# A weight's low three bits: from VectorE's shift-and-merge to a rounded product on GpSimd

## The chip, the cores and the metric

One core of one Trainium2 chip runs the whole program. The metric is the device time of one execution in microseconds, the median over several runs. All times below are in microseconds unless they are marked ns.

## The reference

A causal, exponentially decaying linear attention (no softmax) is followed by a feed-forward layer whose activation is a rational function. Cut to what is computed:

```python
# q, k, v: (8, 8, 576, 64) float32
scores = scale * q @ k^T
ret    = scores * where(rel >= 0, gamma_h ** rel, 0)      # per head
x      = (ret @ v) -> (4608, 512)
# w_in: (512, 2048), w_out: (2048, 512), both float64
h = x @ w_in
g = (a0 + a1*h + a2*h^2 + a3*h^3) / (1 + |b0|*|h| + |b1|*h^2 + 1e-6)
out = (g @ w_out) as float32
```

The weights arrive as float64, eight bytes each, and have to be turned on the chip into numbers that the matmuls can use.

## The kernel before

The 4608 tokens are cut into 36 units of 128 tokens for the attention part and into 9 blocks (`b`) of 512 tokens for the feed-forward part. The feed-forward part runs over 16 slices (`f`) of 128 hidden columns. For each pair (b, f), a *step*, TensorE does `gemm1` (12 matmuls of 128x512 into a PSUM tile `h`) and, three or four steps later, `gemm2` (12 matmuls into accumulators `acc`). Each product of two float32 numbers is made of three products of float32r parts, a high and a low one, which is why each weight tile `w` has two halves.

Between the two matmul groups lies the elementwise work of a step: on ScalarE `ffn_p` (two activations, p and u), `ffn_va`, `ffn_r` (Ln and Exp) and `ffn_hi`; on VectorE a product and a fused product in `ffn_p`/`ffn_p2`, then `ffn_v`, `ffn_q` (two operations) and `ffn_q3`; the low half of g (`ffn_lo`) is made by GpSimd in the first 24 steps and by VectorE later. u lies in SBUF, but in 13 of the first 24 steps it lies in a PSUM tile named `free_at`.

The weights are converted once, by `split_weight`, for 32 slices (16 of `w_in`, 16 of `w_out`). A slice arrives as a tile `bits` of 128 x 512 64-bit words, of which `low` and `high` are the two 32-bit words (every second word). `split_weight` is a generator with four cuts, so that its parts can be spread over the schedule: at `start` ScalarE makes c from the high word by an Abs with a scale; at `split0`, `split1` and `split2` VectorE shifts and merges bits into c; at `split3` ScalarE writes the high half of `w` and GpSimd subtracts it from c for the low half.

The order of the instructions of each engine is the order of the program. It is written out by hand in lists of names, of which `run` calls one after the other:

```python
FIRST = (
    "split1 gemm1 visit ffn_p split2 ffn_p2 ffn_hi decay keep_hi ffn_lo gemm2 ffn_r scale_q split3 decay1 add fade keep_lo"
    " start scale_v split0 ffn_q ffn_q3 ffn_va ffn_v"
).split()
MID = (
    "split1 split2 gemm1 ffn_p ffn_r ffn_hi ffn_lo split3 ffn_va gemm2 ffn_p2 ffn_q ffn_v ffn_q3 start split0"
).split()
```

The stages in order of time: *before* (attention units 0 to 4, ending with the list `LAST_BEFORE`, which ends "split2 split3 split0"; six slices are started there, three of them at its end); steps 0 to 7 and 21 to 23 by `FIRST`; steps 8 to 20 by `MID`; later steps, by other lists, start no slice. `STARTS_BEFORE = [0, 1, 1, 1, 3]` and `STARTS = [1, 1, 2, 1, 2] + [1] * 19` say how many slices are started in each. GpSimd's own order in a step of `FIRST` is `ffn_lo` (tile g), `scale_q` (tile qk, only where a unit follows), `split3` (tile w), `fade` (tile S, only with a unit).

All instructions are recorded by one helper, so that nearly all rows of the profile have its line, L73; they are told apart by their tiles.

Of the kernel before, what the change touches and what calls it, by code (L numbers as in the profile page):

```python
# [15 lines left out]
U32 = mybir.dt.uint32  # L16
I64 = mybir.dt.int64
AF = mybir.ActivationFunctionType
ALU = mybir.AluOpType
# [57 lines left out]
def retention_ffn(ctx: ExitStack, tc: tile.TileContext, qkv, w_in, w_out, ab, masks, gq, gv, out):  # L77
# [26 lines left out]
    pe, act, dve, pool = (InOrder(tc, e) for e in (nc.tensor, nc.scalar, nc.vector, nc.gpsimd))  # L104
# [48 lines left out]
    def split_weight(k):  # L153


        nm = f"{k[0]}_{k[1]}"
        words = bits[k].bitcast(I32).rearrange("p (c w) -> p c w", w=2)
        low, high = words[:, :, 0], words[:, :, 1]
        c = cnv.tile([P, DM], I32, tag="c", name=f"c{nm}")
        cf = c.bitcast(F32)  # L160


        act.activation(cf, high.bitcast(F32), AF.Abs, scale=math.ldexp(1.0, -112))
        yield
        dve.tensor_scalar(c, c, 3, 1, ALU.logical_shift_left, ALU.bitwise_or)
        yield
        dve.scalar_tensor_tensor(c, low, 29, c, ALU.logical_shift_right, ALU.bitwise_or)
        yield
        dve.scalar_tensor_tensor(c, high, -0x80000000, c, ALU.bitwise_and, ALU.bitwise_or)
        yield  # L170
        w = wts.tile([P, 2, DM], F32R, tag=f"w{nm}", name=f"w{nm}")
        del bits[k]
        act.activation(w[:, 0, :], cf, AF.Copy)
        pool.tensor_tensor(w[:, 1, :], cf, w[:, 0, :].bitcast(F32), ALU.subtract)
        parts[k] = w
# [335 lines left out]
    def split_start(n):  # L511
        for k in [k for _, k in zip(range(n), splits)]:
            going.append([split_weight(k), 0])
            next(going[-1][0])
# [129 lines left out]
```

## Time and profile before

| | |
|---|---|
| median of 3 runs | 941.3 us (940.4 to 941.72) |
| the profiled execution: its time | 940.24 us |
| its span in the trace | 938.5 us |
| busy in the span | PE 899.4, DVE 825.0, ACT 710.2, POOL 153.0 us |
| mean clock granted to TensorE | 0.985 |

PE is TensorE's matmuls, PEld its weight loads, DVE is VectorE, ACT ScalarE, POOL GpSimd. In rows of the timeline the columns are the start, the duration, the engine, the line, the operation, output<-inputs, the shapes, the count (xN), and in brackets the idle time of the engine before it with what ended it. In rows of groups the columns after xN are busy time, mean ns of one, then idle time before them. In rows by stage, each engine has its busy time and (in brackets) the number of its instructions, then follow the granted clock of TensorE, the share of the DMA engines that was busy and GB/s.

### The profile page before, as it was taken

The page shows a single profiled execution, that of the slowest core. Times are in us where ns is not written, and L with a number is a line of the kernel's source. Part 1 is how long each engine was busy: PE and PEld are TensorE (multiplying, and loading weights), DVE is VectorE, ACT ScalarE, POOL GpSimd, SP SyncE. Part 2 cuts the span into 40 slices and gives each one's busy share as a digit, 9 for nine tenths or more (in the row PEclk, how much of TensorE's full clock was granted, in tenths as well). Part 3 has the DMA queues.
Part 4 walks back from the last instruction along what each step waited for, and adds up shares of the span by engine and source line. Part 5 has one row for each costly group of instructions (what it writes and reads, how often), then busy time and mean ns, then how long its engine had stood idle before and what let it go on. Part 6 is the DMA issues. An engine that isn't in the chain of part 4 may idle for free.

```text
span 938.5 us, 19369 instructions
## 1 busy us (share of the span) xinstructions
PE 899.4 (96%) x7852; PEld 737.2 (79%) x7852; DVE 825.0 (88%) x1252; ACT 710.2 (76%) x1274; POOL 153.0 (16%) x128
## 2 busy tenths in 40 slices
PE   6689889989999999999999999999999999999997
PEld 6567668877878888888888888888888888888886
DVE  3799999999888888888888999898888888888895
ACT  4567788887777777877787778777877787867775
POOL 3544344444100000000000000000000000000000
PEclk9789999989999999999999999999999999999999
DMA  9976000003212111211121112111211121001001
GB/s 341 362 276 203 1 0 1 1 13 124 91 46 87 49 36 32 84 40 41 43 90 45 47 46 91 45 47 46 90 46 46 45 91 47 1 1 45 1 1 45
DMA packets 20568, 65.50 MB, mean 70 GB/s; under 512 B 2432, under 2 KB 2432, under 8 KB 20480
## 3 DMA queue, kind: packets, MB, share of 16 engines
q1 hardware_dynamic: 20480, 64.28, 19.5%
q8 instruction: 61, 1.00, 0.4%
q14 instruction: 27, 0.22, 0.1%
HBM read 54.83 MB, written 9.44 MB: 68 GB/s over the span
## 4 chain that ended last, share of the span: by engine, by line
PE 46%; DVE 28%; ACT 20%; issue 4%; DMA 1%; POOL 0%; SPq 0%; DVEq 0%; ACTq 0%; POOLq 0%
PE h L73 21%; PE acc L73 20%; DVE p L73 14%; DVE v L73 7%; ACT u L73 6%; ACT v L73 4%; ACT g L73 3%; ACT kv L73 3%; DVE c L73 3%; ACT free_at L73 2%; PE psNone L73 2%; PE ps L73 2%; DVE qk L73 1%; DVE g L73 1%; DVE xlo L73 1%
## 5 line engine op out<-in xcount | busy, mean ns | idle before, releaser
L73 PE MATMUL acc<-w,g 128*128 128x512 f32 x1632 | 399.7, 394 | 5.5 <-ACT o L73 3.6
L73 PE MATMUL h<-xhi,w 128*128 128x512 f32 x1152 | 385.4, 396 | 15.9 <-DVE p L73 15.9
L73 PEld LDWEIGHTS acc<-w,g 128*128 128x128 f32 x1632 | 305.4, 189 | 72.3 <-ACT o L73 4.0
L73 PEld LDWEIGHTS h<-xhi,w 128*128 128x128 f32 x1152 | 219.3, 190 | 69.0 <-DVE p L73 23.0
L73 PE MATMUL h<-xlo,w 128*128 128x512 f32 x576 | 227.0, 394 | 0.0
L73 ACT ACTIVATE p<-h,ab_sb 128x512 f32<-128x512 f32 x144 | 111.2, 772 | 74.8 <-PE h L73 69.6
L73 ACT ACTIVATE u<-h 128x512 f32<-128x512 f32 x131 | 78.0, 596 | 88.8 <-DVE v L73 88.3
L73 DVE SCALAR_TENSOR_TENSOR p<-p,ab_sb,u 128x512 f32<-128x512 f32 x131 | 120.1, 916 | 25.8 <-ACT u L73 20.4
L73 PEld LDWEIGHTS h<-xlo,w 128*128 128x128 f32 x576 | 109.7, 190 | 22.1
L73 DVE TENSOR_TENSOR v<-v,u 128x512 f32<-128x512 f32 x131 | 95.0, 725 | 28.5 <-ACT v L73 28.5
L73 DVE SCALAR_TENSOR_TENSOR p<-p,ab_sb,h 128x512 f32<-128x512 f32 x144 | 107.6, 747 | 4.7
L73 DVE TENSOR_TENSOR p<-p,h 128x512 f32<-128x512 f32 x144 | 98.9, 687 | 14.5 <-ACT u L73 14.2
L73 ACT ACTIVATE v<-u,absb 128x512 f32<-128x512 f32 x131 | 105.2, 803 | 0.5
L73 DVE SCALAR_TENSOR_TENSOR p<-v,p 128x512 f32<-128x512 f32 x144 | 99.6, 691 | 4.5
L73 POOL TENSOR_TENSOR S<-S,gv_sb 128x256 f32<-128x256 f32 x32 | 20.1, 628 | 483.7 <-DVE S L73 480.9
L73 ACT ACTIVATE u<-u,lnb 128x512 f32<-128x512 f32 x131 | 94.9, 724 | 4.3
L73 ACT ACTIVATE g<-p 128x512 fp32r<-128x512 f32 x136 | 85.8, 631 | 12.0 <-DVE p L73 5.4
L73 ACT ACTIVATE u<-v,lnb 128x512 f32<-128x512 f32 x131 | 93.3, 712 | 2.0 <-DVE v L73 2.0
L73 DVE SCALAR_TENSOR_TENSOR v<-v,u 128x512 f32<-128x512 f32 x131 | 91.7, 700 | 0.0
L73 DVE TENSOR_TENSOR g<-p,g 128x512 fp32r<-128x512 f32 x112 | 78.9, 704 | 1.4 <-ACT g L73 1.4
L73 ACT ACTIVATE kv<-kv,gv_sb 128x64 f32<-128x64 f32 x288 | 72.4, 334 | 9.8 <-DMA gv_sb<-in_gv 5.6
L73 POOL TENSOR_TENSOR qk<-qk,gq_sb 128x512 f32<-128x512 f32 x36 | 58.3, 1619 | 55.4 <-DMA qk<-in_qkv 55.4
(72 smaller groups left out, 726.1 us busy)
## 6 DMA issues: line engine op xcount, KB each, us to landing
qk<-in_qkv SPq DMA_DIRECT2D x36, 512.0 KB, 4.0
kv<-in_qkv SPq DMA_DIRECT2D x36, 512.0 KB, 5.6
bits<-in_w_in SPq DMA_DIRECT2D x16, 512.0 KB, 8.8
bits<-in_w_out SPq DMA_DIRECT2D x16, 512.0 KB, 8.2
out<-o SPq DMA_DIRECT2D x16, 512.0 KB, 3.4
out<-o SPq DMA_DIRECT2D x4, 256.0 KB, 2.3
gq_sb<-in_gq SPq DMA_DIRECT2D x1, 256.0 KB, 2.9
mask_sb<-in_masks SPq DMA_DIRECT2D x1, 32.0 KB, 5.1
```

The costliest lines, as they stand in the source:

```text
L73: return lambda *a, **k: self.tc.keep_in_program_order(method(*a, **k))
```

## The change

For each of the 32 slices, the first of VectorE's three operations (c shifted left by three, with a one set in the last place) is taken out. In its place in the program, `split0`, GpSimd reads the low words as unsigned integers, multiplies by 2^-29, takes the smaller of that and 7, and writes the number, rounded to an integer, back over the low words. VectorE's next operation then shifts c left by three itself and merges the number made by GpSimd, where before it shifted the low word right by 29 and merged it into c. The third operation, which merges the sign, is as before.

```diff
         act.activation(cf, high.bitcast(F32), AF.Abs, scale=math.ldexp(1.0, -112))
         yield
-        dve.tensor_scalar(c, c, 3, 1, ALU.logical_shift_left, ALU.bitwise_or)
+        pool.tensor_scalar(low, low.bitcast(U32), math.ldexp(1.0, -29), 7.0, ALU.mult, ALU.min)
         yield
-        dve.scalar_tensor_tensor(c, low, 29, c, ALU.logical_shift_right, ALU.bitwise_or)
+        dve.scalar_tensor_tensor(c, c, 3, low, ALU.logical_shift_left, ALU.bitwise_or)
         yield
         dve.scalar_tensor_tensor(c, high, -0x80000000, c, ALU.bitwise_and, ALU.bitwise_or)
```

## The prediction, made before the changed kernel was run

> **What bounds the kernel now.** I read the page's busy times first, then the chain that ended last, then the span by stages, since conversions take place in the first quarter only.
>
> ```profile
> PE   899.4 (96%) x7852; PEld 737.2 (79%) x7852; DVE 825.0 (88%) x1252; ACT 710.2 (76%) x1274; POOL 153.0 (16%) x128
> ```
> ```profile
> 70.00:90.00 20.00, 18.28 (x249) 14.36 (x248) 18.72 (x29) 15.35 (x30) 9.46 (x9) 1.00 0.55 186
> 90.00:110.00 20.00, 16.41 (x64) 12.74 (x63) 19.26 (x27) 14.08 (x23) 6.98 (x5) 0.91 0.16 53
> 150.00:170.00 20.00, 20.00 (x90) 16.58 (x89) 19.54 (x32) 17.39 (x29) 7.81 (x7) 1.00 0.00 0
> 190.00:215.00 25.00, 22.51 (x244) 18.26 (x243) 24.27 (x37) 18.96 (x41) 12.57 (x9) 0.86 0.14 44
> 540.00:830.00 290.00, 289.70 (x2607) 237.64 (x2596) 259.53 (x396) 225.16 (x398) 24.09 (x21) 1.00 0.15 52
> ```
>
> The first line is the page's (96% and 88% are means over unlike stages), the others the view by stages. In 540:830, where nothing is converted, TensorE has no gap, so there the change is worth nothing. In 90:110 and 190:215 VectorE is busy 19.26 of 20 and 24.27 of 25 us while TensorE has gaps: there a microsecond of VectorE is a microsecond of the run, either way. 150:170 (list `MID`) is a third case, below. GpSimd is never the busy one (7 to 12.6 us), so what it costs must come through what it holds up.
>
> The groups of the operation taken out, of the kind of work put on GpSimd, and the spread of the former over its 32 instructions:
>
> ```profile
> L73 DVE TENSOR_SCALAR c<-c 128x512 int32<-128x512 int32 x32 | 21.9, 693 | 3.6 <-ACT c L73 3.6
> L73 POOL TENSOR_TENSOR w<-c,w 128x512 fp32r<-128x512 f32 x32 | 43.2, 1354 | 20.5 <-ACT w L73 20.5
> L73 POOL TENSOR_TENSOR S<-S,gv_sb 128x256 f32<-128x256 f32 x32 | 20.1, 628 | 483.7 <-DVE S L73 480.9
> L73 DVE TENSOR_SCALAR c<-c x32: 412/424/1497, 18.0 to 204.3; 128x512 int32<-128x512 int32 x32
> ```
>
> The removed operation has a median of 424 ns but a mean of 693 ns. The extra is waiting, and the timeline shows for what:
>
> ```profile
> 110.80 1.38 DVE L73 SCALAR_TENSOR_TENSOR p<-p,ab_sb,u 128x512 f32<-128x512 f32 x1
> 112.10 1.78 DVE L73 SCALAR_TENSOR_TENSOR v<-v,u 128x512 f32<-128x512 f32 x1
> 113.80 0.67 DVE L73 TENSOR_TENSOR v<-v,free_at 128x512 f32<-128x512 f32 x1
> 110.33 1.29 POOL L73 TENSOR_TENSOR g<-p,g 128x512 fp32r<-128x512 f32 x1 [5.04 <-ACT g L73]
> 111.58 1.74 POOL L73 TENSOR_TENSOR w<-c,w 128x512 fp32r<-128x512 f32 x1
> ```
>
> The VectorE operation at 110.80 (two inputs in SBUF) ends at 112.18, 0.56 after GpSimd's g ended at 111.62; GpSimd's w, begun at 111.58, takes 1.74 instead of 1.29, because it waits for that; the next VectorE operation ends 0.56 after w's end at 113.32. The engines take turns, each a whole operation, and VectorE gets going some 0.1 before GpSimd's recorded end (0.56 left of about 0.67). The next, at 113.80, with u in PSUM, takes 0.67. The Trainium skill's "SBUF — State Buffer", section "Who interferes with whom", states this as a lock: a VectorE instruction with two SBUF inputs, or in a two-port mode, and a GpSimd instruction that reads SBUF shut each other out whole. The trace agrees (1.38 and 1.78 us), and the rule speaks against this change.
>
> So the extra of the removed operation (693 against 424 ns) is not saved: it is GpSimd's w, S or qk holding the port, and the next VectorE operation, which has two SBUF inputs too, would wait in its place. What is saved is about 0.42 us and, at times, the wait for ScalarE's c (3.6 us in all). What is paid is the new GpSimd operation's length d, wherever VectorE has only two-input work to do.
>
> **The length d.** No row shows a one-input operation on GpSimd over a tile. Nearest are w, 512 elements from two inputs, 1.29 when nothing is in its way (111.58 is the same form blocked), and S, 256 elements, 0.61 (row at 80.50 below): 2.4 to 2.5 ns per element of two reads, in proportion. The new one has 512 elements and 512 reads. If reads set the time it takes 0.61, like S; if elements do, 1.29, like w. It is no nearer to either by these counts, and has two arithmetic operations and two conversions of type where they have one operation, so I take the middle, 0.95, and keep both ends. The Trainium skill's "GPSIMD Engine Reference", section "Engine selection", calls one-input work on GpSimd roughly line-rate; with the 1.03 cycles per element at 1.2 GHz of its section "Elementwise — side-by-side cycle accounting" that would be an estimated 0.44 us, and the sum at the end of this part would be -1.6 instead of +6.0; no row here shows it.
>
> **The change, stage by stage**, as a function of d.
>
> (1) End of the stage *before*, three slices in a row, where TensorE waits for VectorE:
>
> ```profile
> 35.95 3.67 DVE L73 TENSOR_SCALAR c<-c 128x512 int32<-128x512 int32 x3
> 39.54 1.88 DVE L73 SCALAR_TENSOR_TENSOR c<-bits,c 128x512 int32<-128x512 int32 x3
> 41.35 0.68 DVE L73 TENSOR_TENSOR p<-p,h 128x512 f32<-128x512 f32 x1
> 43.75 0.74 DVE L73 SCALAR_TENSOR_TENSOR p<-p,ab_sb,h 128x512 f32<-128x512 f32 x1
> 36.47 1.45 POOL L73 TENSOR_TENSOR qk<-qk,gq_sb 128x512 f32<-128x512 f32 x1
> 37.88 1.45 POOL L73 TENSOR_TENSOR w<-c,w 128x512 fp32r<-128x512 f32 x1
> 44.54 0.80 PE L73 MATMUL h<-xhi,w 128*128 128x512 f32 x1 [5.18 <-DVE p L73]
> ```
>
> The three removed operations fill 3.67 us, squeezed between qk and w. Without them qk and w take 1.27 and 1.29, w ends near 38.99, and three new ones follow on GpSimd, which is in order: the first ends at 38.95+d. VectorE's first merge now waits for it, but the second new one has already begun, so the merge starts at 38.8+2d; the third new one waits for the merge (0.65) and ends at 39.45+3d; the second merge starts at 39.35+3d, two merges of 0.6 later comes p<-p,h, at 40.55+3d, against 41.35. Cost 3d-0.8: 2.05 at d=0.95, all on the path, since TensorE waits 5.18 for the operation at 43.75.
>
> (2) Steps that start one slice in `FIRST` (five in 1 to 7, three in 21 to 23), by one of them:
>
> ```profile
> 96.81 1.30 POOL L73 TENSOR_TENSOR w<-c,w 128x512 fp32r<-128x512 f32 x1 [1.29 <-ACT w L73]
> 97.33 1.06 DVE L73 TENSOR_SCALAR c<-c 128x512 int32<-128x512 int32 x1
> 98.32 0.74 DVE L73 SCALAR_TENSOR_TENSOR p<-p,ab_sb,u 128x512 f32<-128x512 f32 x1
> 98.98 0.68 DVE L73 SCALAR_TENSOR_TENSOR v<-v,u 128x512 f32<-128x512 f32 x1
> 99.69 0.69 DVE L73 SCALAR_TENSOR_TENSOR p<-v,p 128x512 f32<-128x512 f32 x1
> ```
>
> With the operation at 97.33 gone, p<-p,ab_sb,u waits for w in its place, to about 98.0. The new GpSimd operation stands behind w, waits one turn, and runs from 98.6 to 98.6+d; v<-v,u starts at 98.5+d, against 98.98. Break-even is d=0.48. Where VectorE waited for ScalarE's c (the 3.6 us above, in six places) more is saved: 3.6 over these eight steps is at most 0.45 each. So break-even lies between 0.48 and 0.93; I take 0.70. Cost 8(d-0.70): 2.0 at 0.95.
>
> (3) Two steps with two slices:
>
> ```profile
> 80.50 0.61 POOL L73 TENSOR_TENSOR S<-S,gv_sb 128x256 f32<-128x256 f32 x1
> 80.85 0.88 DVE L73 TENSOR_SCALAR c<-c 128x512 int32<-128x512 int32 x2
> 83.02 0.69 DVE L73 SCALAR_TENSOR_TENSOR p<-v,p 128x512 f32<-128x512 f32 x1
> ```
>
> Without the two operations at 80.85, p<-p,ab_sb,u starts when S lets go, at 81.0; the new operations take the turns behind it and behind v<-v,u (0.65 each), so that p<-v,p starts at about 82.1+2d, against 83.02. Cost 2(2d-0.9): 2.0 at 0.95.
>
> (4) The 13 steps of `MID`:
>
> ```profile
> 152.90 0.77 ACT L73 ACTIVATE v<-free_at,absb 128x512 f32<-128x512 f32 x1
> 155.68 0.58 ACT L73 ACTIVATE free_at<-h 128x512 f32<-128x512 f32 x1 [0.78 <-DVE v L73]
> 152.93 0.75 DVE L73 SCALAR_TENSOR_TENSOR p<-p,ab_sb,h 128x512 f32<-128x512 f32 x1
> 153.71 0.75 DVE L73 SCALAR_TENSOR_TENSOR p<-p,ab_sb,free_at 128x512 f32<-128x512 f32 x1
> 155.56 0.69 DVE L73 SCALAR_TENSOR_TENSOR p<-v,p 128x512 f32<-128x512 f32 x1
> 156.17 0.42 DVE L73 TENSOR_SCALAR c<-c 128x512 int32<-128x512 int32 x1
> 156.62 1.42 DVE L73 SCALAR_TENSOR_TENSOR c<-bits,c 128x512 int32<-128x512 int32 x2
> 152.62 1.30 POOL L73 TENSOR_TENSOR g<-p,g 128x512 fp32r<-128x512 f32 x1 [3.19 <-issue]
> 153.87 1.30 POOL L73 TENSOR_TENSOR w<-c,w 128x512 fp32r<-128x512 f32 x1
> ```
>
> Here ScalarE and VectorE form a loop: ScalarE's free_at waits 0.78 for VectorE's v; and VectorE's p<-p,ab_sb,free_at at 153.71 starts when ScalarE's v of 152.90 is through (153.67), 0.11 later than VectorE's usual 0.66 behind 152.93. The removed operation lies off that loop, between 155.56 and the next p<-p,ab_sb,free_at. So taking out its 0.45 (156.17 to 156.62) shortens nothing; it gives slack of 0.45+0.11. The new operation starts behind w, at 155.13, and holds p<-v,p until 155.01+d, a delay of d-0.55. Up to d=1.12 that is covered; past it each step costs d-1.12.
>
> (5) The slice of step 0 and the first three of *before* lie ahead of waits for other engines; I cost them at nothing (without that cover d-0.5 each, under 2 us).
>
> Sum: 3d-0.8 + 8d-5.6 + 4d-1.8 = 15d-8.2, plus 13(d-1.12) above 1.12. At 0.95 it is +6.0; at 0.61, +1.0; at 1.29, +13.4. The profiled time, 940.24 for a span of 938.5, would become 946.3; the median of 941.3 lies 1.1 above it, so 947.3.
>
> **Rivals.** What this kernel's measurement can tell from no change is 0.2%, about 1.9 us.
>
> A. *Faster: the lock does not hold for one input.* Every blocking row here is of a GpSimd operation with two inputs. If a one-input operation leaves VectorE's second read free, blocks by the new operation vanish: (2) gives -5.6, (3) -1.8, (1) only the wait for the first result, 38.95+0.95 against 39.54, +0.4. Sum -7.0, 934.3. With the lock, a gain beyond 0.2% needs d under 0.42. Against it: VectorE's removed operation, itself of one input, is blocked too (1.06 at 97.33). Chance 0.10.
>
> B. *A short GpSimd operation*: with one input GpSimd is no longer held back by taking turns between two reads and streams as VectorE does, at the removed operation's 0.42 to 0.46: 15d-8.2 = -1.9 to -1.3, about 939.7. For it: half of the reads. Against: 2.4 to 2.5 ns per element now, in S as in w, and more arithmetic. Chance 0.16. (This is the case that the page's line rate means.)
>
> C. *A long one*: conversions of type cost more than the saved read; at d=1.7, 17.3+7.5 = +25, 966; past 1.12 `MID` decides. GpSimd idles 3.19 before each g (152.62), so its own queue still holds. Chance 0.12.
>
> D. *VectorE's delay is hidden in steps 0 to 7 and 21 to 23*, behind TensorE (18.28 of 20 us in 70:90); then only (1) is left, +2.0, 943.3. Against: 19.26 of 20 in 90:110. Chance 0.12.
>
> **The numbers.** My forecast, d between 0.61 and 1.29, +1.0 to +13.4, with 0.95 likeliest: chance 0.50, of which 0.05 within 0.2%. Faster: A 0.10 and a quarter of B, 0.14. Within 0.2%: 0.05, the rest of B 0.12, half of D 0.06: 0.23. Slower: 0.45, C 0.12, half of D 0.06: 0.63. The range leaves out A and most of C (0.18): from 938.5, under B, to 961, d near 1.5. My forecast alone is 942.3 to 954.7.
>
> **What would show it.** d in GpSimd's rows with input `bits`; no TENSOR_SCALAR on VectorE; VectorE's p, v and S rows of 1.0 to 1.8 us more often in 45:112 and 190:215, and p<-p,h of (1) near 43.4; `MID` steps still 5.75 us apart; nothing changed past 220 but the shift. Wrong would be: d under 0.5, or VectorE's two-input rows at 0.68 while GpSimd runs the new operation, or a `MID` step that shortens.

## The result, and the profile after

The changed kernel takes 953.88 us (median; 953.47 to 955.14) beside 941.17 us for the kernel before (940.4 to 941.72): a ratio of 1.0136, 95% interval 1.0124 to 1.0148. That is 12.7 us slower, where 6.0 were forecast. The profiled execution's span is 951.7 us, 13.2 more than before. The ratios below leave out two executions far above the others of their kernel, of 5007 and 1011 us.

The page of the changed kernel, its view by stages, its group of the new operation, the row of that operation by tile (min/median/max in ns), and the row of VectorE's waits for it (us in total, times, longest of them):

```profile
PE 904.5 (95%) x7852; PEld 739.2 (78%) x7852; DVE 815.4 (86%) x1220; ACT 711.6 (75%) x1274; POOL 226.3 (24%) x160
```
```profile
90.00:110.00 20.00, 18.62 (x140) 14.70 (x138) 18.84 (x23) 12.67 (x20) 16.89 (x9) 1.00 0.26 96
150.00:170.00 20.00, 20.00 (x90) 16.57 (x89) 17.25 (x27) 16.80 (x27) 14.04 (x11) 1.00 0.00 1
```
```profile
L73 POOL TENSOR_SCALAR bits<-bits 128x512 int32<-128x512 uint32 x32 | 68.9, 2154 | 2.7
```
```profile
L73 POOL TENSOR_SCALAR bits<-bits x32: 1969/2031/2471, 16.1 to 218.2; 128x512 int32<-128x512 uint32 x32
```
```profile
DVE c L73 <- POOL bits L73: 29.6, 27, 5.0
```

The operation's length d is 2.0 us, twice what was assumed and above the upper end of 1.29. VectorE did lose work (825.0 to 815.4 us), but it stands still for 29.6 us, in 27 of 32 cases, until GpSimd has made the bits. Before, the view of VectorE's waits has no row with GpSimd as what it waited for. In 90:110 GpSimd went from 6.98 to 16.89 of 20 us (the changed kernel is some 9 us later there, so the two windows do not hold quite the same work).

How the 13.2 us gather is seen in the start of one VectorE operation, p<-p,ab_sb,h, in step 0, in step 8 (the first of `MID`) and in step 20 (its last), read from VectorE's timeline of each profiled execution:

| kernel | step 0 | step 8 | step 20 | span |
|---|---|---|---|---|
| before | 43.75 | 110.14 | 181.67 | 938.5 |
| changed | 50.92 | 119.82 | 194.80 | 951.7 |
| later by | 7.2 | 9.7 | 13.1 | 13.2 |

So 7.2 us are lost by step 0, 2.5 in steps 0 to 8, 3.5 in `MID`, and next to nothing past it. TensorE's mean granted clock is lower too (0.976, before 0.985), but the shift does not grow past step 20, and two runs below take 938.7 and 940.8 us at 0.978 and 0.977: the clock does not explain the loss.

**By step 0.** GpSimd, VectorE and TensorE of the changed kernel at the end of the stage before:

```profile
33.54 2.00 POOL L73 TENSOR_SCALAR bits<-bits 128x512 int32<-128x512 uint32 x1
37.34 0.92 POOL L73 TENSOR_TENSOR S<-S,gv_sb 128x256 f32<-128x256 f32 x1 [1.81 <-DVE S L73]
...
39.45 1.27 POOL L73 TENSOR_TENSOR w<-c,w 128x512 fp32r<-128x512 f32 x1
40.80 7.07 POOL L73 TENSOR_SCALAR bits<-bits 128x512 int32<-128x512 uint32 x3
```
```profile
27.97 0.69 DVE L73 SCALAR_TENSOR_TENSOR c<-c,bits 128x512 int32<-128x512 int32 x1 [4.25 <-POOL bits L73]
...
35.57 0.69 DVE L73 SCALAR_TENSOR_TENSOR c<-c,bits 128x512 int32<-128x512 int32 x1 [1.59 <-POOL bits L73]
...
42.81 0.69 DVE L73 SCALAR_TENSOR_TENSOR c<-c,bits 128x512 int32<-128x512 int32 x1 [5.02 <-POOL bits L73]
45.36 0.69 DVE L73 SCALAR_TENSOR_TENSOR c<-c,bits 128x512 int32<-128x512 int32 x1 [1.86 <-POOL bits L73]
47.91 0.69 DVE L73 SCALAR_TENSOR_TENSOR c<-c,bits 128x512 int32<-128x512 int32 x1 [1.85 <-POOL bits L73]
48.52 0.68 DVE L73 TENSOR_TENSOR p<-p,h 128x512 f32<-128x512 f32 x1
```
```profile
51.72 0.80 PE L73 MATMUL h<-xhi,w 128*128 128x512 f32 x1 [10.03 <-DVE p L73]
```

Three results come one after the other, 2.55 apart, and VectorE takes each as it comes. They also start late: GpSimd begins them at 40.80, because the merge at 35.57 had waited 1.59 for the slice before, and VectorE's S, GpSimd's S and GpSimd's w came later in turn (GpSimd's S at 37.34, before at 35.60). TensorE's wait for VectorE's p there grows from 5.18 to 10.03 us.

**Steps 0 to 8**, one of them:

```profile
100.82 2.32 POOL L73 TENSOR_SCALAR bits<-bits 128x512 int32<-128x512 uint32 x1
```
```profile
99.51 1.78 DVE L73 SCALAR_TENSOR_TENSOR v<-v,u 128x512 f32<-128x512 f32 x1
101.33 1.02 DVE L73 SCALAR_TENSOR_TENSOR p<-v,p 128x512 f32<-128x512 f32 x1
102.26 0.68 DVE L73 TENSOR_TENSOR v<-v,u 128x512 f32<-128x512 f32 x1
103.18 0.69 DVE L73 SCALAR_TENSOR_TENSOR c<-c,bits 128x512 int32<-128x512 int32 x1 [0.24 <-POOL bits L73]
```

The GpSimd operation runs from 100.82 to 103.14; its extra 0.33 is the end of VectorE's v<-v,u. p<-v,p, with two inputs in SBUF, is held by 0.33 (1.02 instead of 0.69), and the next v<-v,u, again with two inputs in SBUF, runs its 0.68 in the middle of the GpSimd operation, which I had expected to be impossible. It looks as if the port were shut for the beginning of the operation only: of VectorE's operations in this trace, those held by such a GpSimd operation alone all begin in its first 0.51 us, and lose at most 0.44.

**`MID`**, one step, GpSimd, VectorE and ScalarE:

```profile
153.01 1.30 POOL L73 TENSOR_TENSOR w<-c,w 128x512 fp32r<-128x512 f32 x1
154.39 1.99 POOL L73 TENSOR_SCALAR bits<-bits 128x512 int32<-128x512 uint32 x1
...
163.87 1.29 POOL L73 TENSOR_TENSOR g<-p,g 128x512 fp32r<-128x512 f32 x1 [1.54 <-ACT g L73]
```
```profile
154.92 0.68 DVE L73 SCALAR_TENSOR_TENSOR p<-v,p 128x512 f32<-128x512 f32 x1
156.42 0.69 DVE L73 SCALAR_TENSOR_TENSOR c<-c,bits 128x512 int32<-128x512 int32 x1 [0.81 <-POOL bits L73]
157.14 0.69 DVE L73 SCALAR_TENSOR_TENSOR c<-bits,c 128x512 int32<-128x512 int32 x1
...
159.26 0.75 DVE L73 SCALAR_TENSOR_TENSOR p<-p,ab_sb,free_at 128x512 f32<-128x512 f32 x1
```
```profile
157.93 0.63 ACT L73 ACTIVATE w<-c 128x512 fp32r<-128x512 f32 x1 [0.34 <-DVE c L73]
158.47 0.76 ACT L73 ACTIVATE v<-free_at,absb 128x512 f32<-128x512 f32 x1
```

p<-v,p is not held at all. The merge waits 0.81 for the bits, and ScalarE's copy to w waits for the second merge. ScalarE's v stands behind that copy in its queue, and VectorE's p<-p,ab_sb,free_at waits for v: so the delay reaches the loop that I had called free of it. From there the chain that ended last goes on through VectorE's v, ScalarE's free_at and ScalarE's g to GpSimd's g, which waits 1.54 for it (163.87), and then, in GpSimd's order, through w to the next bits. These need nothing but the loaded word: the order of GpSimd's queue is what ties them into the loop. Once round takes two steps and 12.14 us (p<-p,ab_sb,h starts at 152.27 and 164.41), where two steps took 11.5 before. In the steps by `FIRST`, g is through earlier, and w's wait for ScalarE's copy ties a slice to the one before (1.36 us for the w at 106.35).

### The profile page after: what moved, and what is told of

The parts are those of the page before. It is cut to its first block, busy times and chain, and to the rows that moved or that the text cites. A ratio compares the mean times of both kernels' runs of the same rounds, so it can differ in the third digit from the quotient of the medians.

```text
span 951.7 us, 19345 instructions
## 1 busy us (share of the span) xinstructions
PE 904.5 (95%) x7852; PEld 739.2 (78%) x7852; DVE 815.4 (86%) x1220; ACT 711.6 (75%) x1274; POOL 226.3 (24%) x160
## 4 chain that ended last, share of the span: by engine, by line
PE 72%; DVE 9%; POOL 8%; ACT 5%; issue 3%; DMA 1%; SPq 0%; ACTq 0%; DVEq 0%; POOLq 0%
PE acc L73 34%; PE h L73 33%; POOL bits L73 4%; PE ps L73 3%; DVE p L73 3%; POOL w L73 2%; DVE c L73 2%; DVE v L73 2%; PE y L73 2%; ACT free_at L73 1%; ACT u L73 1%; POOL g L73 1%; DMA bits<-in_w_in 1%; ACT kv L73 1%; ACT v L73 1%
## 5 line engine op out<-in xcount | busy, mean ns | idle before, releaser
L73 DVE SCALAR_TENSOR_TENSOR v<-v,u 128x512 f32<-128x512 f32 x131 | 98.9, 755 | 0.0
```

What stands on the lines that cost most here:

```text
L73: return lambda *a, **k: self.tc.keep_in_program_order(method(*a, **k))
```

## The experiments

Two theories. *Waiting*: the loss is VectorE waiting for a 2.0 us result that starts late on GpSimd; the port costs some 0.4 us an operation. *Port*: the loss is VectorE's two-input operations shut out of the port. Ratios are to the kernel before on the same chip.

**The relief alone.** The changed kernel without GpSimd's operation; `nought` is a constant zero:

```diff
-        pool.tensor_scalar(low, low.bitcast(U32), math.ldexp(1.0, -29), 7.0, ALU.mult, ALU.min)
...
-        dve.scalar_tensor_tensor(c, c, 3, low, ALU.logical_shift_left, ALU.bitwise_or)
+        dve.scalar_tensor_tensor(c, c, 3, nought, ALU.logical_shift_left, ALU.bitwise_or)
```

> The changed kernel with the GpSimd operation left out: VectorE's two operations stay, the second input of the first is a constant zero, so the lowest three bits of each weight are zero. This prices the relief of VectorE by itself. Both theories (waiting for GpSimd's result, or GpSimd shutting VectorE out of the port) take the cost of the change from the GpSimd operation, so both expect less than the 941.2 us of before: 2 to 9 us less, 932 to 939, nearly all of it before 115 us and after 185 us, and MID steps still 5.75 us apart. If the loss came from the new form of VectorE's merge or from TensorE's clock alone, the time would stay above 945.

Measured: ratio 0.993 (0.9913 to 0.9947), 6.6 us faster. p<-p,ab_sb,h starts at 41.56, 104.16 and 175.60 in the three steps: 2.2 saved by step 0, 3.8 in steps 0 to 8, 0.1 in `MID`, and 1.9 more past it in the profiled execution (span 930.5). So VectorE's shorter work is worth 6.6 us, next to none of it in `MID`, and the GpSimd operation costs 19 us against that (12.7 and 6.6).

**The operation without anyone waiting for it.** The kernel before with it added, for the first 16 slices:

```diff
         dve.tensor_scalar(c, c, 3, 1, ALU.logical_shift_left, ALU.bitwise_or)
+        if count[0] < 16:
+            count[0] += 1
+            pool.tensor_scalar(spill, low.bitcast(U32), math.ldexp(1.0, -29), 7.0, ALU.mult, ALU.min)
```

> The kernel before, all three VectorE operations kept, and for the first 16 of the 32 slices the same GpSimd operation besides, at the same place, written to a tile that nobody reads. Nothing waits for its result. Theory 'waiting' (the port is shut only while GpSimd reads, some 0.45 us, and the loss is VectorE waiting for a result that takes 2.0 us): at most 16 x 0.45 = 7 us more than before, likely 2 to 5, 943 to 946. Theory 'port' (VectorE's two-input operations are shut out for all of the 2.0 us): 16 x (2.0 - 0.1) less what falls into idle time, 15 to 30 us more, 956 to 971.

Measured: 1.0057 (1.0042 to 1.0072), 945.5 us. The 16 operations, 2.1 us each, cost 5.1 us, 0.3 each, where *port* needed 15 or more. Step 0 is not moved at all (43.75), though three of them run one after the other beside the merges in front of it:

```profile
39.07 2.36 DVE L73 SCALAR_TENSOR_TENSOR c<-bits,c 128x512 int32<-128x512 int32 x3
```

These three took 1.88 before. Of the 5.1 us, 4.0 are lost in steps 0 to 8, where ten of the operations run (step 8 starts at 114.16, before at 110.14). There the relief saves 3.8, and the change still loses 2.5: of the 6.3 us that the operation costs in these steps, up to 4 are its presence (the port, or GpSimd's next operations coming later; this run does not part the two), and the rest is left for the waiting.

**Where the loss lies.** The first six slices by the old operations; and the other way round, only the 13 slices of `MID` by the new ones:

```diff
+        if count[0] < 6:
+            count[0] += 1
+            dve.tensor_scalar(c, c, 3, 1, ALU.logical_shift_left, ALU.bitwise_or)
+            yield
+            dve.scalar_tensor_tensor(c, low, 29, c, ALU.logical_shift_right, ALU.bitwise_or)
+        else:
...
```

> The changed kernel, but the six slices started in the stage before are converted by VectorE's three operations as in the kernel before. In the trace of the changed kernel, VectorE's p<-p,ab_sb,h of step 0 comes 7.2 us later than before (50.92 against 43.75), and the shift grows by 2.5 us up to the first MID step, by 3.6 in MID, and no more after. So 'waiting' expects 7 us back: 946.5, with steps 1 to 7 and MID as slow as in the changed kernel. 'Port' expects 5 us back (its 3d-0.8 at d=2.0), 948.7. If later stages make up for or hide the shift, less than 3 us come back.

```diff
+        count[0] += 1
+        if not 16 < count[0] <= 29:
+            dve.tensor_scalar(c, c, 3, 1, ALU.logical_shift_left, ALU.bitwise_or)
...
+        else:
...
```

> Only the 13 slices started in MID are converted the new way, the 19 others as in the kernel before. Nothing is saved in MID in any theory (its loop over ScalarE does not hold the removed operation), and its steps go from 5.75 to 6.0-6.05 us because VectorE's merge, ScalarE's copy to w and with it the next slice wait for a 2.0 us result behind w: 3.3 to 4 us more than before, 944 to 945. If the MID steps of the changed kernel were slow only because of what came before them, it is 941.

Measured: the first, 1.0061 (1.0044 to 1.0078), some 7 us back by the two ratios; its step 0 is at 43.60 again, and steps 0 to 8 and `MID` lose 2.4 and 4.4. The second, 1.0056 (1.0042 to 1.0069), 945.5 us, 5.3 more than before, above the 3.3 to 4 expected. `MID` alone loses 4.8 us of it (110.96 to 187.32 from step 8 to 20, 76.4 against 71.5). In the changed kernel it lost 3.5; the difference lies in two steps, 8 to 9 (7.68 against 7.30) and 13 to 14 (7.16 against 6.20). Why these two are shorter in the changed kernel I did not find out.

```profile
DVE c L73 <- POOL bits L73: 8.9, 13, 0.8
```

This row of VectorE's waits in the `MID`-only run shows the wait by itself: 13 slices, 13 waits, 0.7 each, of which the removed operation's 0.45 pays back a part.

**A shorter operation.** The changed kernel with `7.0, ALU.mult, ALU.min` cut to `None, ALU.mult`:

> The changed kernel with the minimum left out, so that GpSimd's operation has one arithmetic step (1.58 us instead of 2.0 in the run of forms) and one in sixteen weights may get a wrong low bit. Only its length changes. 'Waiting': three results in a row before step 0 come 3 x 0.43 earlier, two single ones 0.43 each, so 1.3 to 2.2 us there; 13 MID steps get back the 0.28 to 0.45 us each that they lost: 3.6 to 5; together 5 to 7 us less than the change, 947 to 949. 'Port while it reads' alone (reading as long as before) expects no more than 1 us less, 953.

Measured: 1.0072 (1.0058 to 1.0086), 946.85 us. That is 6 us less than the change by the two ratios. Its operation, held times included, has a mean of 1710 ns against 2154:

```profile
L73 POOL TENSOR_SCALAR bits<-bits 128x512 int32<-128x512 uint32 x32 | 54.7, 1710 | 2.7
```

p<-p,ab_sb,h of step 0 comes 2.2 earlier than in the changed kernel (48.69), the steps to 8 win 1.6, `MID` 0.9 and the later steps 0.9 (5.6 in the two spans). The waits for bits fall to 18.8 us in 20 cases. `MID` gave back less than its 3.6 to 5, the other stages more: the sum falls where *waiting* had it, its parts do not.

**What sets its length.** Eight forms of it on an unused tile, in late steps of the kernel before:

> The kernel before, with eight variants of the GpSimd operation, four instructions each, on a tile that is otherwise unused, in late steps where GpSimd is idle and VectorE has two-input work. a: as in the change (unsigned in, integer out, every second word, two operations). b: float to float, every second word. c: as a, contiguous. d: float to float, contiguous. e: as d, one operation. f: signed in. g: unsigned in, float out, every second word. h: float in, integer out. Theory 'conversions make it long': a, c and f near 2.0 us, b and d near 0.8 to 1.3, g and h between. Theory 'stride': a and b near 2.0, c and d below 1.3. Theory 'two operations by the element': a to d all near 2.0 and e near 1.0. On the port: 'waiting' expects VectorE's two-input operations that meet a probe to be held at most some 0.5 us, so none above 1.3; 'port' expects some of them at 1.8 to 2.7 us.

The groups of a (as in the change), d (float, contiguous) and e (as d, one operation), then the GpSimd timeline with two of d in a row and three of c in a row, and VectorE beside those of c:

```profile
L73 POOL TENSOR_SCALAR va__4200<-va__4200 128x512 int32<-128x512 uint32 x4 | 8.9, 2234 | 0.3
...
L73 POOL TENSOR_SCALAR vd__5610<-vd__5610 128x512 f32<-128x512 f32 x4 | 8.4, 2107 | 0.3
L73 POOL TENSOR_SCALAR ve__6275<-ve__6275 128x512 f32<-128x512 f32 x4 | 6.4, 1595 | 0.3
```
```profile
499.18 6.66 POOL L73 TENSOR_SCALAR vc__5242<-vc__5242 128x512 int32<-128x512 uint32 x3
...
524.82 4.02 POOL L73 TENSOR_SCALAR vd__5610<-vd__5610 128x512 f32<-128x512 f32 x2
```
```profile
499.57 1.09 DVE L73 SCALAR_TENSOR_TENSOR p<-p,ab_sb,u 128x512 f32<-128x512 f32 x1
500.59 0.68 DVE L73 SCALAR_TENSOR_TENSOR v<-v,u 128x512 f32<-128x512 f32 x1
...
503.98 1.10 DVE L73 TENSOR_TENSOR v<-v,u 128x512 f32<-128x512 f32 x1
```

All forms with two arithmetic operations have means from 2.11 to 2.25 us, whatever their types and strides; two of d back to back take 4.02, so 2.0 each when not held. One operation takes 1.6. So neither the conversions nor the stride made it long. Of the theories only the third comes near: the second operation costs 0.4 us (2.0 less 1.6), but most of the time stays with one, so that e is not 1.0. All forms have 512 elements, so how the time grows with the elements no run shows. And beside the 6.66 us of GpSimd's three operations, VectorE's operations are held by 0.35 (1.09 against 0.74) and 0.41, or not at all.

**Earlier, in front of w.** Each operation is issued a step earlier, ahead of w in GpSimd's queue (name `low` put before `split3` in `FIRST` and `MID`, before w in the stage before too):

```diff
-        pool.tensor_scalar(low, low.bitcast(U32), math.ldexp(1.0, -29), 7.0, ALU.mult, ALU.min)
+    def make_low(k):
+        low = bits[k].bitcast(I32).rearrange("p (c w) -> p c w", w=2)[:, :, 0]
+        pool.tensor_scalar(low, low.bitcast(U32), math.ldexp(1.0, -29), 7.0, ALU.mult, ALU.min)
...
-    "split1 split2 gemm1 ffn_p ffn_r ffn_hi ffn_lo split3 ffn_va gemm2 ffn_p2 ffn_q ffn_v ffn_q3 start split0"
+    "split1 split2 gemm1 ffn_p ffn_r ffn_hi ffn_lo low split3 ffn_va gemm2 ffn_p2 ffn_q ffn_v ffn_q3 start split0"
```

> The changed kernel with every GpSimd operation on low words issued one step earlier, and in GpSimd's order in front of the previous slice's w instead of behind it; the same 32 operations, on the same data. 'Waiting': VectorE's 29.6 us of waits for bits nearly vanish, MID steps go back to 5.75 us, and what is left is the port for some 0.45 us per operation against the relief of 0.42: 938 to 943. 'Port': the operations are as long and meet the same VectorE work, so no more than 3 us come back: 950 to 954.

Measured: 1.0079 (1.0058 to 1.01), 948.5 us. A miss: the waits for bits are gone, and yet `MID` steps take 6.33 us, and `MID` loses 6.7 us against before. GpSimd and VectorE:

```profile
151.58 2.00 POOL L73 TENSOR_SCALAR bits<-bits 128x512 int32<-128x512 uint32 x1
153.65 1.74 POOL L73 TENSOR_TENSOR w<-c,w 128x512 fp32r<-128x512 f32 x1
```
```profile
154.16 1.78 DVE L73 SCALAR_TENSOR_TENSOR c<-c,bits 128x512 int32<-128x512 int32 x1
```

w, which does hold the port for its length, was moved back by the 2.0 us, out of the time in which VectorE reads u from PSUM (153.87 before) and onto the merge, which now takes 1.78. The port does cost, through the neighbour that was moved.

**Earlier, behind w.** The same, but `low` stands after `split0`, where the change has its operation, for the slice of the next step; the first six slices are converted the old way:

> In the run that issued the GpSimd operations a step ahead in front of w, VectorE's waits for bits were gone, but w came 2.0 us later and met VectorE's merge (1.78 instead of 0.69). Here the operation stays behind w, where the change has it, but works for the slice of the next step; the six slices of the stage before are converted the old way. Theory 'waiting plus port while it reads': no waits for bits, MID steps back at 5.75 us, steps 1 to 7 and 21 to 23 at relief (3 to 4 us) less port (3 to 4 us): 939 to 942.5, the same as before. If the operation's mere presence on GpSimd (the queue, the port for 2.0 us) costs, MID stays above 5.9 us a step and the time is 944 or more.

Measured: 0.9984 (0.9975 to 0.9993), 938.7 us: 1.5 us faster than the kernel before and, by the two ratios, 14 us faster than the change.

```profile
155.90 1.99 POOL L73 TENSOR_SCALAR bits<-bits 128x512 int32<-128x512 uint32 x1
```
```profile
153.31 0.75 DVE L73 SCALAR_TENSOR_TENSOR p<-p,ab_sb,h 128x512 f32<-128x512 f32 x1
154.40 0.75 DVE L73 SCALAR_TENSOR_TENSOR p<-p,ab_sb,free_at 128x512 f32<-128x512 f32 x1 [0.35 <-ACT v L73]
...
156.26 0.83 DVE L73 SCALAR_TENSOR_TENSOR p<-v,p 128x512 f32<-128x512 f32 x1
157.02 0.68 DVE L73 SCALAR_TENSOR_TENSOR c<-c,bits 128x512 int32<-128x512 int32 x1
...
159.06 0.75 DVE L73 SCALAR_TENSOR_TENSOR p<-p,ab_sb,h 128x512 f32<-128x512 f32 x1
```

The operation is 2.0 us long as ever; the merge does not wait, the `MID` step is 5.75 again (153.31 to 159.06), and VectorE has 0.35 us to spare in front of p<-p,ab_sb,free_at, waiting for ScalarE.

**All 32 of them ahead and behind w**, the first six included:

> As the run with the operation behind w and a step ahead, but with the first six slices by GpSimd too, issued so that all but one of them are done before VectorE asks. 'Waiting plus port while it reads': VectorE's p<-p,ab_sb,h of step 0 at 43 to 45 (43.75 before, 50.92 with the change), the rest as in the other run: 938.5 to 944. If the three results in a row at the end of that stage still come late, 945 to 948.

Measured: 1.0004 (0.9995 to 1.0013), 940.8 us: no change. Step 0's p<-p,ab_sb,h starts at 44.94; one wait of 4.4 us for bits is left, before step 0. So of the 19 us that the operation costs in the change, some 12 are gone when its result is made a slice ahead, with the operation and its place behind w as they were. The other 7, about what the relief saves, are its presence and that one wait.

## Why the prediction was wrong in size

The direction was right: the kernel became slower, by 12.7 us where +6.0 was forecast. By its steps:

**The length d: the term that was mis-sized.** 0.95, with 0.61 and 1.29 as ends, against 2.0 measured. The ends were taken from operations with two inputs and one arithmetic operation, as if inputs and elements alone set the time. The runs show the second arithmetic operation at 0.4 us, and 1.6 us for one input and one operation, more than the 1.29 of two inputs. An upper end from another instruction of the engine was no bound. The estimate of 0.44 us from the Trainium skill's "GPSIMD Engine Reference" (sections "Engine selection" and "Elementwise — side-by-side cycle accounting") is further off still.

**That VectorE pays d at the port: wrong.** With d=2.0 the formula 15d-8.2+13(d-1.12) gives +33, against 12.7. For w and g the rows of before hold (the other engine waits for the whole operation), but the one-input operation holds VectorE by less than half a microsecond (0.44 at most in the changed kernel). The rule of the Trainium skill's "SBUF — State Buffer", section "Who interferes with whom", that the pair is locked for the whole instruction, does not hold for it: 102.26 runs at 0.68 inside it. The prediction's own sign of this, VectorE's two-input rows at 0.68 while GpSimd runs the new operation, came true. Rival A had this half right. The formula's part without the operation, -8.2, is near what the relief alone measured, -6.6. So two errors of opposite sign, half the length and too long a hold, made a forecast that looks nearer than its working was: that it came within 7 us was luck.

**The wait for the result** was in the working of stage (1) alone. There 3d-0.8 gives 5.2 at d=2.0, against 7.2; nearly all of the missing 2.0 is (5), the first three slices, costed at nothing with a bound of under 2 us: the merges of two of them waited 4.25 and 1.59, and GpSimd's three operations began at 40.80 instead of 38.95. VectorE made up for the first wait (its xlo before the next merge starts at 33.28, before at 33.21), but that wait made GpSimd's w late (32.18, before 30.03), and the third slice's bits stand behind that w. In `MID`, (4), I let the operation end wherever it would and looked only at p<-v,p; the measured delay goes merge, ScalarE's w, ScalarE's v, and closes through GpSimd's g and w. That the removed operation is off `MID`'s loop, and that its removal saves nothing there, was right (0.1 us in the run of relief alone). In (2) and (3) the forecast was 4.0, and at d=2.0 the terms give 16.6; measured are 2.5 in steps 0 to 8 and about 0.1 past `MID`, as the short hold would have it.

**Rivals.** C had the length (1.7 was its example) but with `MID` deciding by the port; the time it gave, 966, is 12 too much. D has the small loss of steps 0 to 8 (2.5 us) but not its reason: VectorE's delay is not hidden there, since the relief saves 3.8 and the unread operations cost 4.0 in the same steps. B is refuted by the length.

## What to carry to other kernels

Price a moved operation on its new engine by that form itself, or keep the range open upwards; elements and inputs of another form do not bound it. Then ask first not what it shuts out but who waits for it, and what stands ahead of it in its engine's queue: here the change with the same 32 operations of 2.0 us made the kernel 12.7 us slower with each behind w for the same slice, no slower with each made for the slice after, and 7.4 us slower (by the ratio) with each ahead of w, where it pushed a neighbour onto other work.

## What the runs showed of the hardware

On GpSimd, an operation of a tile with constants (128x512) takes 2.0 us with two arithmetic operations and 1.6 with one, for integer or float and for every word or every second (the eight forms, and the run with the shorter operation), while one of two tiles takes 1.3 (w, 1.29). Over its length it holds VectorE's two-input operations by 0.46 us at most in the traces looked at (the changed kernel, the unread operations, the run behind w from the seventh slice on), where GpSimd's two-input operations hold them up to their whole length (1.78 instead of 0.68). Why the longer one lets go sooner, the profile does not show.
